# Query-major exponentials of an attention backward pass by DMA transpose instead of a second matmul and exp

## The chip, the cores and the metric

The kernel runs on one core of a Trainium2 chip. The metric is the device time of one execution in microseconds (us), as the median of several runs. Before the change it is 2852.1 us, from two runs of 2850.25 and 2853.94 us.

## What is computed

A block of a network with its gradients. The forward part is `out = x + s * g`, where `s` is multi-head attention (32 heads of width 16, 2048 rows, model width 512) on the layer-normed input, and `g` is the SiLU of a two-layer MLP. The kernel returns `out` and the gradients with respect to `x` and the six weights and biases, for a given gradient of `out`. All inputs and outputs are bf16.

```
xn = layernorm(x)
q, k, v = split(xn @ wqkv)                       # 32 heads of 16
p = softmax(q @ k.T / 4)                         # 2048 x 2048 for each head
s = (p @ v) @ wo
g = silu(gelu(layernorm(xn) @ w1 + b1) @ w2 + b2)
out = x + s * g
grads = vjp of out for (x, wqkv, wo, w1, b1, w2, b2)
```

The change touches the attention's part alone. Its backward pass needs the matrix of exponentials in two orientations. With keys on the partitions ("key-major") it serves the sums over keys: the output, the row sums and the gradient of q. With queries on the partitions ("query-major") it serves the sums over queries: the gradients of k and v.

## The kernel before, in words

There are three phases: `phase_pre` (norms, MLP, projections; the first attention step follows at about 285 us), `attention_core`, and `phase3` (weight gradients; from about 2257 us). `attention_core` is emitted in an order written out by hand (a manual schedule), and each engine runs its own instructions in that order.

**Loops.** Two heads are worked on at a time, so there are 16 pairs. For each pair there are four query chunks `qc` of 512 queries: 64 blocks `j`. Each block has 16 steps `kb`, one for each 128 keys: 1024 steps `g`, and 19 more at the end to drain. Sixteen steps after the key-major work of a block ("a unit") its query-major work ("b unit") runs: also 16 units, numbered by a key chunk `kc` of 512 keys and a query group `qb` of 128 queries. The Z matmuls of a b unit come another `lagb` = 3 steps later.

**The a unit of a step.** L648 `s`: two matmuls of scores into a PSUM tile. L676 `et`: ACT's exponential of both heads into a bf16 tile that holds four steps (`etp`, 3 tiles). L662 `d`: two matmuls. L697 `gts`: VectorE multiplies `d` by `et` into a tile that holds two steps (`gtp`, 4 tiles). L729, L732, L744: matmuls that sum over keys into `X`. Every second step, L710: SyncE (SP) issues one DMA transpose of the whole `gts` tile, 128x2048, into half of a `gk` tile (`gbp`).

**The b unit of a step.** L634 `t`: two matmuls of the same scores with the queries on the partitions. L684 `e`: ACT's exponential of them. L807: Z matmuls with `e`. L813: Z matmuls with `gk`. After the fourth `qb` of a `kc`, L818 or L820 adds Z to `acc`. For the units named in `dma_units`, here (1, 3) and (3, 3), two of the 16, `t` and `e` are left out: after the last of the four steps that fill an `et` tile, L716 issues a DMA transpose of a quarter of it, 128x1024, into an `ek` tile (`ekp`), and L807 reads that instead.

**Queues.** All DMAs of this phase go through SP's queue: L710, L716, and for each pair the loads L585 to L587, the transposes L594 and L602 of the operands KVT and QDT, and the store L827. SP issues in order, and a transpose that has to wait holds up those behind it. A tile of a pool is written again when its last reader is done. In the order of emission, `emit_dmat(g)` stands ahead of `emit_z(g - lagb, ...)` in a step, so a step's transposes are emitted before its Z matmuls.

Of the kernel before, what the change touches and what calls it, by code (L numbers as in the profile page):

```python
# [541 lines left out]

def attention_core(ctx, tc, NAT_s, NATQ_s, Oall, dQall, dKVT_out, ident_f32, npairs=16, nqc=4):
    nc = tc.nc
    dma_units = ((1, 3), (3, 3))
    lagb = 3
    sb = lambda name, bufs: ctx.enter_context(tc.tile_pool(name=name, bufs=bufs))
    opnd = sb("opnd", 1)
# [3 lines left out]
    ps_z = ctx.enter_context(tc.tile_pool(name="ps_z", bufs=1, space=PSUM))  # L552
    etp = sb("etp", 3)
    gtp = sb("gtp", 4)
    gbp = sb("gbp", 6)
    ekp = sb("ekp", 4)
    ep = sb("ep", lagb + 2)
    xsp = sb("xsp", 1)
    finp = sb("finp", 2)
# [306 lines left out]
def full_kernel(ctx, tc, A_x, A_wqkv, A_wo, B_x, B_w1, B_b1, B_w2, B_b2, grad_out,  # L866
# [32 lines left out]
    with ExitStack() as cO:  # L899
        pO = cO.enter_context(tc.tile_pool(name="persistO", bufs=1))  # L900
        k.Oall = pO.tile([128, NT, D], bf16, name="Oall")
        k.dQall = pO.tile([128, NT, D], bf16, name="dQall")
        if "att" in phases:
            with ExitStack() as cB:
                with tc.manual_schedule():
                    attention_core(cB, tc, k.NAT_s, (k.NATQq_s, k.NATQd_s), k.Oall, k.dQall, k.dKVT_s, k.ident_f)
        if "3" in phases:
            phase3(ctx, tc, k, A_x, A_wqkv, A_wo, B_w1, B_w2, grad_out, out_0, out_1, out_2, out_3, out_4, out_5, out_6, out_7, dbg)
# [56 lines left out]
```

## Time and profile before

The profiled execution has a span of 2849.1 us; the median of the runs is 2852.1 us.

| engine, whole span | busy us | share | instructions |
|---|---|---|---|
| PE (matmul) | 2397.8 | 84% | 19712 |
| PE weight loads | 845.8 | 30% | 19712 |
| DVE (VectorE) | 2029.7 | 71% | 3382 |
| ACT (ScalarE) | 2057.1 | 72% | 2357 |
| POOL (GpSimd) | 619.0 | 22% | 1023 |

| DMA issue in attention | count | size of one | issue, median us | start of issue to landing, median us |
|---|---|---|---|---|
| gk <- gts, L710 | 512 | 128x2048 bf16 | 1.93 | 4.4 |
| ek <- et, L716 | 128 | 128x1024 bf16 | 1.80 | 3.9 |

How to read the lines that follow: the page cuts the span into 40 equal slices of 71 us and gives the busy share of each in tenths, where 9 means 90% or more. "DMA" is the share of the core's 16 DMA engines. A row of the groups gives line, engine, operation, output<-input, shapes and count, then busy time and the mean duration of one in ns, then the engine's idle time just ahead of these instructions and what ended most of it. The stages view gives for each stretch the busy time and count of each engine, then the granted clock of TensorE, the DMA share, and GB/s.

### The profile page before, as it was taken

What the parts mean: (1) busy time and instruction counts of PE and PEld (TensorE: products, weight loads), DVE (VectorE), ACT (ScalarE), POOL (GpSimd) and SP (SyncE); (2) the same over time, 40 slices, a digit from 0 to 9 for tenths busy, and PEclk for the clock granted to TensorE, in tenths of its full rate; (3) what the DMA queues carried; (4) which work ended last, traced back from release to release, by engine and by line L of the source; (5) the groups of instructions that cost most, each with busy time, mean ns of one, the idle gap of its engine ahead of it and who ended that gap; (6) DMA issues with size and microseconds to landing.
All of it is one profiled execution on the core that took longest, in us unless ns stands there. A gap on an engine that the chain in (4) does not pass through costs nothing. (4 is left out here: it accounts for less than half of the span.)

```text
span 2849.1 us, 50869 instructions
## 1 busy us (share of the span) xinstructions
PE 2397.8 (84%) x19712; PEld 845.8 (30%) x19712; DVE 2029.7 (71%) x3382; ACT 2057.1 (72%) x2357; POOL 619.0 (22%) x1023
## 2 busy tenths in 40 slices
PE   3686999999999999999999999999999857665967
PEld 2332222222222222222222222222222333332443
DVE  5664778878878878878877877888888638880044
ACT  2342799999999999999999999999999634440020
POOL 0434101111111110101101111110101227870024
PEclk8898799999999999999999999999999978887989
DMA  5434889999999999999899999999999753326431
GB/s 177 107 126 128 156 161 184 159 179 172 167 180 159 181 166 174 174 164 182 156 182 171 167 183 154 183 168 170 177 164 159 191 164 103 97 83 160 115 130 42
DMA packets 1426198, 442.86 MB, mean 155 GB/s; under 512 B 1349281, under 2 KB 1410082, under 8 KB 1425954
## 3 DMA queue, kind: packets, MB, share of 16 engines
q1 hardware_dynamic: 1352562, 385.98, 72.9%
q10 hardware_dynamic: 73392, 53.62, 6.2%
q8 instruction: 154, 2.52, 0.3%
q14 instruction: 90, 0.74, 0.1%
HBM read 65.41 MB, written 55.32 MB: 42 GB/s over the span
## 5 line engine op out<-in xcount | busy, mean ns | idle before, releaser
L697 DVE TENSOR_TENSOR gts<-d,et 128x512 bf16<-128x512 f32 x2048 | 1315.0, 683 | 374.6 <-ACT et L676 146.4
L676 ACT ACTIVATE et<-s 128x1024 bf16<-128x1024 f32 x1024 | 1058.1, 1056 | 11.8 <-PE d L662 11.7
L684 ACT ACTIVATE e<-t 128x1024 bf16<-128x1024 f32 x896 | 933.9, 1043 | 165.0 <-PE t L634 163.9
L662 PE MATMUL d<-QDT,KVT 32*128 32x512 bf16 x2048 | 492.4, 382 | 30.5 <-DVE gts L697 28.5
L648 PE MATMUL s<-QDT,KVT 32*128 32x512 bf16 x2048 | 402.9, 385 | 135.7 <-ACT et L676 120.3
L729 PE MATMUL X<-et,Lc 128*32 128x512 bf16 x2048 | 405.3, 392 | 14.1 <-DVE xs L750 14.1
L732 PE MATMUL X<-et,NAT 128*32 128x512 bf16 x2048 | 405.5, 393 | 0.0
L744 PE MATMUL X<-gts,NAT 128*17 128x512 bf16 x2048 | 400.7, 388 | 0.0
L813 PE MATMUL Z<-gk,W 128*32 128x512 bf16 x2048 | 394.2, 379 | 0.0
L807 PE MATMUL Z<-e,W 128*32 128x512 bf16 x1792 | 351.3, 387 | 2.8 <-DVE acc L820 2.0
L634 PE MATMUL t<-KVT,QDT 32*128 32x512 bf16 x1792 | 349.9, 382 | 2.3 <-ACT e L684 2.3
L777 POOL TENSOR_TENSOR W<-NATQd,rL 128x128 bf16<-128x128 bf16 x64 | 25.7, 401 | 1386.0 <-DVE rL L772 1386.0
L648 PEld LDWEIGHTS <-KVT 32*128 32x128 bf16 x2048 | 146.9, 91 | 399.3 <-issue 397.8
L634 PEld LDWEIGHTS <-QDT 32*128 32x128 bf16 x1792 | 103.9, 91 | 365.7 <-issue 365.7
L744 PEld LDWEIGHTS <-NAT 128*17 128x17 bf16 x2048 | 93.0, 88 | 338.5 <-issue 338.5
L729 PEld LDWEIGHTS <-Lc 128*32 128x32 bf16 x2048 | 104.3, 93 | 216.2 <-issue 216.2
L820 DVE TENSOR_TENSOR acc<-Z,acc 64x512 f32<-64x512 f32 x192 | 129.0, 672 | 13.0 <-PE Z L813 13.0
L807 PEld LDWEIGHTS <-W 128*32 128x32 bf16 x2048 | 121.3, 93 | 55.3 <-issue 53.8
L662 PEld LDWEIGHTS <-KVT 32*128 32x128 bf16 x2048 | 108.1, 91 | 9.4 <-issue 1.0
L825 POOL CAST ob<-acc 64x512 bf16<-64x512 f32 x64 | 38.7, 605 | 313.3 <-DVE acc L820 311.3
L813 PEld LDWEIGHTS <-W 128*32 128x32 bf16 x2048 | 103.9, 96 | 7.5
L732 PEld LDWEIGHTS <-NAT 128*32 128x32 bf16 x2048 | 99.3, 94 | 14.5
(200 smaller groups left out, 2600.2 us busy)
## 6 DMA issues: line engine op xcount, KB each, us to landing
gk<-gts SPq DMA_TRANSPOSE x512, 4.4
HG_s<-hg SPq DMA_DIRECT2D x16, 448.0 KB, 3.0
DH_s<-dh ACTq DMA_DIRECT2D x16, 448.0 KB, 2.5
NAT<-NAT_s SPq DMA_DIRECT2D x16, 264.0 KB, 3.1
GB_s<-gB ACTq DMA_DIRECT2D x16, 256.0 KB, 2.0
dKVT_s<-ob SPq DMA_DIRECT2D x16, 256.0 KB, 3.8
dhc<-DH_s ACTq DMA_DIRECT2D x2, 2048.0 KB, 13.9
w_sb<-in_B_w_dram SPq DMA_DIRECT2D x2, 1792.0 KB, 14.8
```

Of the source, the lines that this page charges most:

```text
L634: nc.tensor.matmul(t[:, hj, :], lhsT=op["QDT"][r:r + 32, q0:q0 + 128], rhs=op["KVT"][r:r + 32, kc * 512:(kc + 1) * 512], start=True, stop= ...
L648: nc.tensor.matmul(s[:, hj, :], lhsT=op["KVT"][r:r + 32, kb * 128:(kb + 1) * 128], rhs=op["QDT"][r:r + 32, qc * 512:(qc + 1) * 512], start ...
L662: nc.tensor.matmul(d[:], lhsT=op["KVT"][r:r + 32, kb * 128:(kb + 1) * 128], rhs=op["QDT"][r:r + 32, qc * 512:(qc + 1) * 512], start=True, ...
L676: nc.scalar.activation(out=et[:, :, kb % 4, :, :].rearrange("k b h q -> k h b q"), in_=st_s.pop(g)[:].rearrange("k h (b q) -> k h b q", b= ...
L684: nc.scalar.activation(out=e[:], in_=st_t.pop(g)[:], func=ACT.Exp)
L697: nc.vector.tensor_tensor(out=gts[:, kb % 2, hj, :].rearrange("k (b q) -> k b q", b=4), in0=ds[hj][:].rearrange("k (b q) -> k b q", b=4), ...
L729: nc.tensor.matmul(X[64 + 32 * hj:96 + 32 * hj, :], lhsT=Lc[:], rhs=et[:, :, kb % 4, hj, :], start=(kb == 0), stop=False, skip_group_check ...
L732: nc.tensor.matmul(X[32 * hj:32 * hj + 32, :], lhsT=NATt[:, kb, hj, 1:33], rhs=et[:, :, kb % 4, hj, :], start=(kb == 0), stop=(kb == 15), ...
L744: nc.tensor.matmul(X[64 + 32 * hj:64 + 32 * hj + 17, :], lhsT=NATt[:, kb, hj, 0:17], rhs=gts[:, kb % 2, hj, :], start=False, stop=(kb == 1 ...
L807: nc.tensor.matmul(Z[32 * hj:32 * hj + 32, :], lhsT=blk[j]["W1"][:, qb, hj, :], rhs=ev[:, hj], start=(qb == 0), stop=False, tile_position= ...
L813: nc.tensor.matmul(Z[32 * hj:32 * hj + 32, :], lhsT=blk[j]["W2"][:, qb, hj, :], rhs=gv[:, :, :, hj, qb, :], start=False, stop=(qb == 3), t ...
L820: nc.vector.tensor_tensor(out=av, in0=Z[0:64, :], in1=av, op=ALU.add)
```

## The change

Three lines of `attention_core`. `dma_units` now names all 16 units of a block, so `emit_t` and `emit_exp_b` do nothing (L634 and L684 have no instruction any more), `emit_dmat` issues four `ek` transposes after each fourth step instead of one after each eighth, and all Z matmuls of L807 read `ek`. The pool `ekp` grows from 4 to 20 tiles and `gbp` shrinks from 6 to 5. The pool `ep` stays, unused. The arithmetic is otherwise the same.

```diff
 def attention_core(ctx, tc, NAT_s, NATQ_s, Oall, dQall, dKVT_out, ident_f32, npairs=16, nqc=4):
     nc = tc.nc
-    dma_units = ((1, 3), (3, 3))
+    dma_units = tuple((kc, qb) for kc in range(4) for qb in range(4))
     lagb = 3
...
     etp = sb("etp", 3)
     gtp = sb("gtp", 4)
-    gbp = sb("gbp", 6)
-    ekp = sb("ekp", 4)
+    gbp = sb("gbp", 5)
+    ekp = sb("ekp", 20)
     ep = sb("ep", lagb + 2)
```

## The prediction

> **What bounds the kernel now.** I read the page's slices first, then the costliest groups, then the busy time by stretch, and last the DMA queues of the attention stage alone. All durations are from one profiled execution with a span of 2849.1 us; the median of the runs is 2852.1, so I add 3 us at the end.
>
> The slices, and from the groups the rows that the change touches:
> ```profile
> PE   3686999999999999999999999999999857665967
> DVE  5664778878878878878877877888888638880044
> ACT  2342799999999999999999999999999634440020
> DMA  5434889999999999999899999999999753326431
> GB/s 177 107 126 128 156 161 184 159 179 172 167 180 159 181 166 174 174 164 182 156 182 171 167 183 154 183 168 170 177 164 159 191 164 103 97 83 160 115 130 42
> ...
> L697 DVE TENSOR_TENSOR gts<-d,et 128x512 bf16<-128x512 f32 x2048 | 1315.0, 683 | 374.6 <-ACT et L676 146.4
> L676 ACT ACTIVATE et<-s 128x1024 bf16<-128x1024 f32 x1024 | 1058.1, 1056 | 11.8 <-PE d L662 11.7
> L684 ACT ACTIVATE e<-t 128x1024 bf16<-128x1024 f32 x896 | 933.9, 1043 | 165.0 <-PE t L634 163.9
> ...
> L634 PE MATMUL t<-KVT,QDT 32*128 32x512 bf16 x1792 | 349.9, 382 | 2.3 <-ACT e L684 2.3
> ...
> gk<-gts SPq DMA_TRANSPOSE x512, 4.4
> ```
> Attention runs from about 288 to 2257 us: 1969 us, 1043 steps, 1.89 us each. PE, ACT and the DMA engines all show 9 there, so three candidates stand side by side. The stretches separate them (columns: busy of PE, weight load, DVE, ACT, POOL; granted clock, DMA share, GB/s). First the whole stage; then a stretch in which DMAs are queued up without a pause; then one that holds a single gk transpose; then one with gk, ek, gk in a row:
> ```profile
> 288.00:2257.00 1969.00, 1798.09 (x16395) 549.96 (x16395) 1566.56 (x2626) 1789.68 (x1921) 267.14 (x699) 0.99 0.97 171
> 575.40:607.88 32.48, 30.04 (x277) 9.07 (x278) 26.00 (x44) 29.29 (x32) 3.04 (x9) 1.00 1.15 195
> ```
> ```profile
> 1228.70:1231.40 2.70, 2.48 (x22) 0.64 (x20) 2.43 (x5) 1.92 (x3) 0.00 (x0) 1.00 1.02 194
> 1232.30:1239.00 6.70, 5.88 (x54) 1.93 (x51) 6.33 (x14) 6.01 (x7) 2.74 (x8) 1.00 1.05 198
> ```
> ACT is what sets a step today: it is busy 1790 of 1969 us, 91% (its instructions overlap by about a tenth, so the two groups' sum, 1992, is larger), and the waits of L676 sum to 11.8 us. PE is close behind. The DMA engines are nearer to their end than anything says in words: the share of 0.97 is a sum of packet times that overlap, so it is not the ceiling. In the queued-up stretch the same column reads 1.15, at 195 GB/s, and other such stretches of 32 to 43 us read 192 to 196 GB/s. **That is the ceiling: about 195 GB/s.** The stage moves 171, 88% of it. The reader should take two things from this: ACT is the limit by a small margin, and the resource to which the change moves the work has one eighth left.
>
> **What the Trainium skill says.** "Advanced Engine Details and Errata", section X-Bar Transpose (TRN2), expects 350-400 GB/s of a transposing DMA; "DMA: Bandwidth & Descriptors", section Latency and other measured facts, has 261 GB/s with a non-contiguous middle dimension. The trace agrees with neither: 195 GB/s, in packets of which 1,349,281 of 1,426,198 are under 512 B. The measurement decides; the pages' figures serve as a rival below. "Perfetto Trace Analysis", section DMA Instruction — HWDGE, says that a DMA instruction's time in the profile ends with its issue and that the movement lies outside it; the trace agrees: a gk's issue takes 1.93 us in the median and it lands 4.4 us after its start.
>
> **The change part by part.**
> - Removed, PE: 1792 matmuls of L634, 349.9 us, with their weight loads. PE in the stage goes from 1798 to 1448 us. Worth nothing on the end if DMA is the bound.
> - Removed, ACT: 896 exponentials of L684, 933.9 us. What stays in the stage is L676, at most 1058 us. This was the limit, so the next one is what counts: DVE, 1567 us of work, all of it kept; PE 1448; and DMA.
> - Added, DMA: ek transposes from 128 to 1024, so 896 x 128x1024 bf16 = 896 x 262,144 B = 234.9 MB, all on SP's queue. The DMA view cut to the stage says 336.73 MB now, of which some 4.7 MB are loads of the next stage that start in its last 15 us: 332 + 235 = 567 MB. At 195 GB/s that is 2907 us. **This is the path.** Nothing covers it: the DMA engines already were at 88%, and the work beside it (DVE 1567) is far shorter.
> - The same from single transposes: the 194 GB/s x 2.70 us above are 524 KB, one gk, so at most 2.7 us and by its packets 2.6; gk, ek, gk fit in 6.7 us, so an ek adds about 1.4. Four steps need 2 gk and 4 ek: 2 x 2.6 + 4 x 1.37 = 10.7 us, against 4 x 1.89 = 7.5 us now. 256 such groups make 2739; the KVT and QDT transposes of 15 pairs 30 x 2.6 = 78; their loads 15 x 0.54 MB / 195 = 42; 16 stores 22; total 2881. The 16 KB instruction fetches that ride on the same engines (128 in the stage) are in the first sum, not in this one. The two agree within 1%. I take 2905.
> - Unknown: an ek behind an ek does not occur before. From below, half a gk in a run of gk (2.46 / 2 = 1.23); from above, SP's issue time, 1.80 us median plus 0.09 between two, 1.89. Unhindered issues of 1.25 occur with the queue full, so issue can keep pace; I take 1.37. The ends change the stage by 768 x (-0.14) = -108 and, SP limited, see the second rival.
> - gbp 6 to 5: a gk tile is claimed at step 4m+1, and the tile five earlier is last read by Z at step 4m+2, one step later. So SP's first gk of a group waits for PE, and the second gk and the four ek's of that group are queued behind it. It costs nothing while compute is ahead of the DMAs by over a step, and it will be: gts has 4 tiles of two steps and et 3 of four, so the engines may lead by a whole group of transposes before they block. If compute did not lead, it would cost a step and the 1.2 us from issue to first packet.
> - ekp 4 to 20: five groups of 4; a tile's last Z read is one step ahead of its reuse. No wait.
> - Late next: DVE and ACT will stand idle for their buffers, L697 for gts and L676 for et, both freed by transposes. Z reads its ek 16 steps after it was made, so PE does not wait there.
>
> Sum: outside the stage 2849.1 - 1969 = 880; stage 2905; the first packets start some 4 us into it, and the tail has no t and e any more, -5. Span 3784 to 3800, plus 3: **3800 us**.
>
> **Rivals.**
> 1. *SP's issuing is the bound.* For: medians of 1.80 (ek) and 1.93 (gk). A group takes 4 x 1.89 + 2 x 2.02 = 11.6 us, 2970 for all, with loads and stores 3060; total 880 + 3060 = 3940. Against: issues of 1.25 to 1.32, and where they are longer, they end with the transfer ahead.
> 2. *The gk wait bites:* SP stands until PE has done the later step, and the DMA engines run dry once a group: up to 256 x (1.6 + 1.2) = 717 more, 4500. Against: the lead worked out above.
> 3. *Faster:* the transposes run at the pages' 350-400 GB/s when fed without pause. Then 567 MB take 1420 to 1620 us, DVE sets the stage at 1567 to 1700, and the kernel takes 2450 to 2600. It is decided by one number: over 567 / 1969 = 288 GB/s the change gains, under it it loses. At 261 it would be 3055. Against: between 1216 and 1246 us, taken by half microseconds, none with queued transposes shows over 222 GB/s, but for a microsecond of catch-up after a stall (266).
> 4. *The change leaves t and e in place:* ruled out, since in the changed program no instruction stands at L634 or L684.
>
> **How the numbers follow.** Transfer-bound near 195 GB/s (3680 to 3880): 0.74. SP bound or a mix with it (3880 to 4050): 0.16. Gk wait or other gaps (over 4050): 0.05. Pages' rates: 0.05, of which 0.03 faster. The range 3680 to 3980 holds the first case and most of the second. A measurement of this kernel can tell about 2% from no change; nothing lies near that line, so same gets 0.01.
>
> **What would show it.** Right: GB/s near 190-200 through all of the stage, DMA share at about 1.15 throughout, ACT down to some 3 or 4 tenths and DVE to 5, the step at 2.8 us, L697 and L676 idle behind DMA. SP bound: GB/s under 185 with ek issues at 1.8 us end to end. Gk wait: holes in the DMA traffic once in four steps and SP waiting for PE at L710. I am wrong if the stage's rate leaves 185 to 205 GB/s, or if DVE stays busy over 70% of it.

## The result, and the profile after

The changed kernel takes 3826.6 us in the median (3825.1 to 3828.1), against 2852.1 us: a ratio of 1.342, with a 95% interval of 1.338 to 1.346. The profiled execution has a span of 3823.3 us. The forecast was 3800 us, with a range of 3680 to 3980.

The slices of the page of the changed kernel, and four of its costliest groups:
```profile
PE   5777767776767676767777777777777776676678
ACT  3433333333333333333333333333333332344020
PEclk8986777776777877777777777777776777888889
DMA  5349999999999999999999999999999999432641
GB/s 166 108 127 185 194 192 193 196 193 194 193 193 194 194 195 195 195 195 195 196 192 195 194 194 192 195 195 195 193 192 196 193 195 208 152 97 82 157 142 38
...
L697 DVE TENSOR_TENSOR gts<-d,et 128x512 bf16<-128x512 f32 x2048 | 1312.7, 683 | 1259.6 <-DMA gk<-gts 939.7
L676 ACT ACTIVATE et<-s 128x1024 bf16<-128x1024 f32 x1024 | 1005.4, 1023 | 1899.2 <-PE d L662 1111.4
...
L662 PE MATMUL d<-QDT,KVT 32*128 32x512 bf16 x2048 | 785.1, 497 | 539.6 <-DVE gts L697 529.0
...
L807 PE MATMUL Z<-ek,W 128*32 128x512 bf16 x2048 | 518.0, 501 | 10.9 <-DMA ek<-et 8.2
```
The GB/s row was uneven before, between 154 and 191 in the slices of attention. Now it stands at 192 to 196 in nearly all of them, as a resource at its ceiling would. L697 waited 375 us before, 257 of them for ACT or PE; it now waits 1260 us, and 940 of them end with the landing of a gk, which frees a `gts` tile. L807, which reads the new ek tiles, waits 11 us in all. So no consumer is late; the producers stand still for their buffers.

The same stage in the stages view (columns as before: PE, weight load, DVE, ACT, POOL; clock, DMA share, GB/s), and the waits of SP's own queue (total, times, longest):
```profile
288.00:3216.00 2928.00, 2101.88 (x14593) 479.80 (x14594) 1567.95 (x2621) 1002.55 (x1022) 268.35 (x698) 0.74 1.09 194
```
```profile
SPq L710 <- PE d L662: 222.8, 141, 3.3
...
SPq L710 <- PE s L648: 129.2, 53, 3.5
SPq L716 <- ACT et L676: 115.6, 167, 2.0
SPq L710 <- PE X L744: 69.8, 48, 2.3
```
The span grew by 974 us: 959 of it in the attention stage (2928 against 1969), 15 in the phase after it. DVE's work in the stage is what it was, 1568 us; ACT's fell from 1790 to 1003. SP does wait for PE at L710, 422 us in all, where the kernel before has no such wait; the prediction worked it out for the smaller `gbp`, which was not tried apart. But in the records of the DMA packets of the stage, the gaps of over 0.1 us between packets come to 12 us altogether (207 us in the kernel before): the queued transfers cover that wait.

The same records show what the 194 GB/s is made of. For 159 us of the stage, in 197 stretches of mostly about 1 us, packets still come but the rate, averaged over 0.25 us, is under 40 GB/s. Of the 175 fetches of instructions by DMA in the stage, 170 have such a stretch begin within 2.5 us of them, though these 2.5 us cover only 15% of the stage. So the rate is a mean with stalls in it, most of them beside an instruction fetch; whether the fetch is the cause was not tried. The first gk of a group, the one that waits for PE, has 36 us of these stalls, and the second, which does not, has 28: little room for a cost of that wait.

### The profile page after: what moved, and what is told of

Same layout as the page of the kernel before. It is cut to its first block, busy times and chain, and to the rows that moved or that the text cites. A ratio compares the mean times of both kernels' runs of the same rounds, so it can differ in the third digit from the quotient of the medians.

```text
span 3823.3 us, 47091 instructions
## 1 busy us (share of the span) xinstructions
PE 2709.7 (71%) x17920; PEld 779.4 (20%) x17920; DVE 2035.0 (53%) x3382; ACT 1272.9 (33%) x1461; POOL 621.5 (16%) x1023
## 5 line engine op out<-in xcount | busy, mean ns | idle before, releaser
L697 DVE TENSOR_TENSOR gts<-d,et 128x512 bf16<-128x512 f32 x2048 | 1312.7, 683 | 1259.6 <-DMA gk<-gts 939.7
L676 ACT ACTIVATE et<-s 128x1024 bf16<-128x1024 f32 x1024 | 1005.4, 1023 | 1899.2 <-PE d L662 1111.4
L662 PE MATMUL d<-QDT,KVT 32*128 32x512 bf16 x2048 | 785.1, 497 | 539.6 <-DVE gts L697 529.0
L729 PE MATMUL X<-et,Lc 128*32 128x512 bf16 x2048 | 540.5, 523 | 181.1 <-ACT et L676 177.4
L648 PE MATMUL s<-QDT,KVT 32*128 32x512 bf16 x2048 | 492.6, 477 | 109.5 <-ACT et L676 96.0
L732 PE MATMUL X<-et,NAT 128*32 128x512 bf16 x2048 | 529.8, 511 | 0.0
L807 PE MATMUL Z<-ek,W 128*32 128x512 bf16 x2048 | 518.0, 501 | 10.9 <-DMA ek<-et 8.2
L813 PE MATMUL Z<-gk,W 128*32 128x512 bf16 x2048 | 524.0, 505 | 0.0
L744 PE MATMUL X<-gts,NAT 128*17 128x512 bf16 x2048 | 515.7, 499 | 0.2 <-DVE gts L697 0.2
L662 PEld LDWEIGHTS <-KVT 32*128 32x128 bf16 x2048 | 126.7, 95 | 579.1 <-issue 578.6
L807 PEld LDWEIGHTS <-W 128*32 128x32 bf16 x2048 | 123.9, 98 | 37.9 <-issue 27.6
L813 PEld LDWEIGHTS <-W 128*32 128x32 bf16 x2048 | 114.8, 106 | 17.0 <-issue 15.7
L762 DVE COPY xt<-XT 128x512 f32<-128x512 f32 x64 | 44.3, 692 | 89.2 <-PE XT L760 89.2
L427 PE MATMUL ps_dy<-w1T,dh1T 128*128 128x512 bf16 x224 | 75.1, 477 | 1.0 <-ACT dh1T L422 0.3
```

What stands on the lines that cost most here:

```text
L427: nc.tensor.matmul(ps[:], lhsT=dh1T[:, fc, :], rhs=w1T[:, fc, :], start=(fc == 0), stop=(fc == FC - 1))
L648: nc.tensor.matmul(s[:, hj, :], lhsT=op["KVT"][r:r + 32, kb * 128:(kb + 1) * 128], rhs=op["QDT"][r:r + 32, qc * 512:(qc + 1) * 512], start ...
L662: nc.tensor.matmul(d[:], lhsT=op["KVT"][r:r + 32, kb * 128:(kb + 1) * 128], rhs=op["QDT"][r:r + 32, qc * 512:(qc + 1) * 512], start=True, ...
L676: nc.scalar.activation(out=et[:, :, kb % 4, :, :].rearrange("k b h q -> k h b q"), in_=st_s.pop(g)[:].rearrange("k h (b q) -> k h b q", b= ...
L697: nc.vector.tensor_tensor(out=gts[:, kb % 2, hj, :].rearrange("k (b q) -> k b q", b=4), in0=ds[hj][:].rearrange("k (b q) -> k b q", b=4), ...
L729: nc.tensor.matmul(X[64 + 32 * hj:96 + 32 * hj, :], lhsT=Lc[:], rhs=et[:, :, kb % 4, hj, :], start=(kb == 0), stop=False, skip_group_check ...
```

## The experiments

Two questions were put to the chip. Is it the transfers' bytes that set the 2928 us, or SP's issuing, or the wait of the first gk? And was ACT really what bounded the kernel before, as the prediction read it?

### e1: half of the units

```diff
-    dma_units = tuple((kc, qb) for kc in range(4) for qb in range(4))
+    dma_units = tuple((kc, qb) for kc in range(4) for qb in (1, 3))
-    ekp = sb("ekp", 20)
+    ekp = sb("ekp", 10)
```


> Eight of the 16 units of a block go by transpose, the other eight keep t and e (ekp 10). Transfer theory: 512 fewer ek transposes are 134 MB less, so (566 - 134) MB at 194.8 GB/s give a stage of about 2220 us and a kernel of 3110 us (3080 to 3140), still well over the 2852 of before, with 192 to 197 GB/s in the stage. Rival, SP's issuing: a group of four steps issues 2 x 1.42 + 2 x 2.33 = 7.5 us, 1920 us in all, which the exponentials hide: about 2870 us. Rival, the gk wait or the lower TensorE clock: nearly all of the loss stays, over 3500 us.

Measured: 3124.5 us, 1.096 (1.091 to 1.101) of the kernel before. Its stage:
```profile
288.00:2520.00 2232.00, 1919.25 (x15573) 494.20 (x15573) 1553.33 (x2619) 1479.62 (x1529) 266.43 (x696) 0.89 1.12 194
```
Same 194 GB/s, fewer bytes, a stage of 2232 us: the time follows the bytes. The three rivals that foresaw 2870 or over 3500 us fall. But the number of transposes falls with the bytes here; e2 and e3 change the one without the other.

### e2: one transpose where there were four

```diff
-            for qb in range(4):
-                if (kc, qb) in dma_units:
-                    ek = ekp.tile([128, 8, 128], bf16, name="ek")
-                    blk[j]["Ek"][(kc, qb)] = ek
-                    nc.sync.dma_start_transpose(out=ek[:], in_=st_et[g][:, qb]...)
+            ek = ekp.tile([128, 4, 8, 128], bf16, name="ek")
+            for qb in range(4):
+                blk[j]["Ek"][(kc, qb)] = ek
+            nc.sync.dma_start_transpose(out=ek[:]..., in_=st_et[g][:]...)
```
`ekp` is 5 here, and L807 reads its quarter of the long tile.

> The four ek transposes of an et tile are issued as one of 128x4096: same bytes, 256 issues in place of 1024. Transfer theory with bytes alone: no change from 3826 us (3780 to 3830). Transfer theory with a fixed part in each transpose (an ek takes 1.39, a gk 2.50 us, so 0.28 fixed): 768 x 0.28 = 215 less, 3610 us. SP's issuing as the bound: 768 x 1.42 = 1090 us of issue time less, under 2900 us unless the long issue grows in proportion.

Measured: 3680.3 us, 1.291 (1.285 to 1.297). The stage, and the issue of the long transpose (min/median/max in ns):
```profile
295.00:3070.00 2775.00, 2041.79 (x14554) 471.45 (x14548) 1562.33 (x2617) 1003.34 (x1020) 267.58 (x698) 0.76 1.14 204
```
```profile
L715 SPq DMA_TRANSPOSE ek<-et x256: 4726/5194/6365, 297.8 to 3065.5; - x128
```
The bytes are the same and 146 us are gone, 0.19 us for each of the 768 seams between transposes that no longer exist; the rate rises from 194 to 204 GB/s. That lies between the two transfer expectations. The run does not decide against SP's issuing, though. The expectation set a condition, "unless the long issue grows in proportion", and it did: 5.19 us in the median, 3.9 times the 1.33 us of a single ek in the changed kernel. So the 0.19 us may belong to the data or to SP.

### e3: the same count, half the bytes

```diff
-                    ek = ekp.tile([128, 8, 128], bf16, name="ek")
-                    nc.sync.dma_start_transpose(out=ek[:], in_=st_et[g][:, qb]...)
+                    ek = ekp.tile([128, 4, 128], bf16, name="ek")
+                    nc.sync.dma_start_transpose(out=ek[:], in_=st_et[g][:, qb, 0:2]...)
```
Each matmul of L807 becomes two of 256 columns that both read that half, so the other half is missing from the sum; where qb = 0, L813 now comes first.

> Still 1024 ek transposes, but each moves half (128x512), so 134 MB less; the Z matmuls read that half twice, so part of the sum is left out, in four matmuls of 256 columns in place of two of 512. Transfer theory: with bytes alone 3826 - 134 MB / 194.8 GB/s = 3137 us; with 0.28 us fixed in each, 1024 x 0.555 less, 3260 us. If the issue of 1.25 + 0.09 us becomes the floor of these short ones: 4 x 1.34 + 2 x 2.0 = 9.4 us a group, 3300 to 3400 us. SP's issuing as the bound of the changed kernel: no change, 3826 us.

Measured: 3742.6 us, 1.313 (1.307 to 1.319). **None of the four numbers was right.** The stage, then a stretch with two gk and the start of the first ek, then one with the last three ek of a group; below, the issue of an ek:
```profile
292.00:3133.00 2841.00, 2049.84 (x16616) 608.34 (x16611) 1565.45 (x2619) 1013.24 (x1021) 267.49 (x698) 0.76 0.84 152
1007.00:1012.60 5.60, 3.39 (x36) 0.95 (x32) 2.89 (x5) 2.95 (x3) 0.06 (x1) 0.97 1.11 210
1012.70:1016.60 3.90, 3.90 (x39) 1.19 (x36) 2.80 (x6) 1.02 (x1) 0.61 (x1) 0.62 0.50 101
```
```profile
L716 SPq DMA_TRANSPOSE ek<-et x1024: 1198/1264/2509, 296.9 to 3131.9; - x171
```
The same row of the changed kernel:
```profile
L716 SPq DMA_TRANSPOSE ek<-et x1024: 1233/1330/2882, 295.2 to 3212.7; - x171
```
The DMA share says it: 1.11 while gk are moved, 0.50 while ek are. In the packets of the second stretch an ek of 128x512 flows for 0.77 us and one starts every 1.31 us, which is the issue of 1.26 and the step to the next. So these short transposes are paced by SP. The group comes to more than the 9.4 us that I had worked out because I let SP issue ahead during the gk's; it does not get far ahead. The first ek of a group is issued only when the second gk is already being moved, and the others after it, so the 2.5 us of each gk and the 1.31 us of each ek come one after the other. For the changed kernel this means that its ek's (1.40 us from end to end behind one another) lie only 0.09 us above this issue floor: **transfers and SP's issuing are nearly in balance there**. That the transfers are ahead by this little is seen in the packets: in the changed kernel an ek starts to flow before the ek ahead of it has ended in 761 of 768 cases, in e3 in 23. Halving the bytes of the ek's alone took 84 us off, where the bytes alone would have taken 689.

### e4: no gk

```diff
-            nc.sync.dma_start_transpose(out=blk[j]["Gk"][kc][:, h], ...)   # L710
-            nc.tensor.matmul(Z[...], lhsT=blk[j]["W2"][...], rhs=gv[...])  # L813
```


> The changed kernel without the gk transposes and without the Z matmuls that read them: that part of the sum is left out. 268 MB less, 298 MB are left. Transfer theory: the DMA engines need 298 / 0.195 = 1530 us and are no longer alone; DVE's 1573 us of work sets the stage at 1650 to 1800, the kernel at 2530 to 2700 us, and DVE is busy over 85% of the stage. If something other than transfers set the 2925 us (ek issues of 1.42 us x 1024 = 1454 us do not, nor do they here), such as the lower TensorE clock, the kernel stays over 3300 us.

Measured: 2541.0 us, 0.892 (0.886 to 0.897). The stage:
```profile
288.00:1945.00 1657.00, 1484.38 (x12581) 321.89 (x12580) 1540.81 (x2631) 1048.01 (x1028) 268.14 (x699) 0.95 1.05 183
```
This kernel leaves out the part of the sum that the gk carry. DVE is busy 1541 of 1657 us, 93%: with half the bytes taken off, the engine that the prediction named as the next bound is nearly full. But 183 GB/s is nearly all that ek's alone allow, since a 128x1024 every 1.40 us is 187 GB/s; the run does not tell the two apart. All 1024 ek transposes are still there.

### e5, e6, e7: none, three and four units by transpose

These are the kernel before with `dma_units` changed, to test what bounded it:
```diff
-    dma_units = ((1, 3), (3, 3))
+    dma_units = ()                                    # e5
+    dma_units = ((0, 3), (1, 3), (3, 3))              # e6, ekp 6
+    dma_units = ((0, 3), (1, 3), (2, 3), (3, 3))      # e7, ekp 6
```


> The kernel before with no unit by transpose (dma_units empty): 128 exponentials and 256 t matmuls more, 33.5 MB less to move. If ACT bounds the kernel before: 128 x 0.92 to 1.04 = 118 to 133 us more, 2970 to 2985 us. If the DMA engines already bound it: faster, about 2850 - 33.5 / 0.195 = 2680 us or at least not slower.

> The kernel before with three units of 16 by transpose (ekp 6). ACT bound: 64 exponentials less, 59 to 67 us less, 2785 to 2793 us, as the DMA engines would need only (332 + 17) / 0.195 = 1790 us. DMA engines already in the way through their bursts: 2840 to 2930 us.

> The kernel before with four units of 16 by transpose, one for each key chunk (ekp 6). ACT bound: 118 to 133 us less, but the DMA engines then need (332 + 34) / 0.195 = 1875 us of a stage of 1969, so at best 2852 - 94 = 2758; I expect 2760 to 2820 us. If the transfers' waits already cost: no gain, 2850 to 2900 us.

The stage with none and with four units:
```profile
288.00:2257.00 1969.00, 1804.90 (x16651) 566.57 (x16651) 1573.47 (x2624) 1892.21 (x2048) 268.00 (x699) 0.99 0.85 154
288.00:2257.00 1969.00, 1788.07 (x16115) 532.21 (x16115) 1560.15 (x2621) 1680.48 (x1790) 266.77 (x697) 0.99 1.07 188
```
Measured: 2850.3 us (0.9995 of the kernel before, 0.9988 to 1.0002), 2850.7 us (0.9993, 0.9980 to 1.0006) and 2848.7 us (0.9987, 0.9977 to 0.9996). **Between none and four units the time moves by 0.1% at most**, though ACT's work in the stage goes from 1892 us of 1969 (96%) with none to 1680 with four. ACT's work alone therefore does not set the time with two units; at none, with 96%, it may, which no run shows. The rows of e, in the attention stage, for none, two (the kernel before) and four units show where the saved exponentials went:
```profile
L684 ACT ACTIVATE e<-t 128x1024 bf16<-128x1024 f32 x1024 | 1082.7, 1058 | 63.4 <-PE t L634 63.0
```
```profile
L684 ACT ACTIVATE e<-t 128x1024 bf16<-128x1024 f32 x896 | 933.9, 1043 | 165.0 <-PE t L634 163.9 <-ACT et L676 0.2
```
```profile
L684 ACT ACTIVATE e<-t 128x1024 bf16<-128x1024 f32 x768 | 793.5, 1033 | 274.8 <-PE t L634 274.8
```
Each exponential left out adds (274.8 - 63.4) / 256 = 0.83 us of waiting for the next t. The order of PE around such a step in the kernel before shows why (start, duration, instruction):
```profile
1214.01 0.39 PE L648 MATMUL s<-QDT,KVT 32*128 32x512 bf16 x2
1214.16 0.37 PE L662 MATMUL d<-QDT,KVT 32*128 32x512 bf16 x1
1214.76 0.37 PE L662 MATMUL d<-QDT,KVT 32*128 32x512 bf16 x1 [0.23 <-DVE gts L697]
1215.06 0.39 PE L744 MATMUL X<-gts,NAT 128*17 128x512 bf16 x2
1215.35 0.39 PE L807 MATMUL Z<-e,W 128*32 128x512 bf16 x2
1215.56 0.39 PE L813 MATMUL Z<-gk,W 128*32 128x512 bf16 x2
1215.89 0.39 PE L634 MATMUL t<-KVT,QDT 32*128 32x512 bf16 x2
```
The step has no t of its own. Its second d waits for DVE to free a PSUM buffer, and the next step's t stands behind it, X and Z on PE and comes at 1215.89. ACT had nothing to do for 0.78 us before the e at 1216.38, most of the 0.9 us that it had saved.

### e8, e9, e10: the next t ahead of d

If that is the cause, moving one matmul pair ahead of d, X and Z must free the time. This edit is on the kernel before, with two, three and four units:
```diff
-        emit_t(g)
+        if g not in st_t:
+            emit_t(g)
...
         emit_s(g + 1)
+        b = b_unit(g)
+        if b is not None and b[1:] in dma_units:
+            emit_t(g + 1)
         emit_d(g)
```


> The kernel before (two units of 16 by transpose), with one matmul pair moved: in a step whose own unit has no t, the next step's t is emitted ahead of d instead of after z. Theory: what a left-out exponential saves on ACT (0.9 us) is paid back because the next t stands on PE behind d, and d waits for gts on DVE to free its PSUM buffer; moved ahead, t is there in time, the 164 us in which L684 waits for t fall under 80, and up to 128 x 0.8 = 100 us go: 2750 to 2800 us. Rival: the pace is DVE's or PE's own, and the wait only moves to another row: 2840 to 2860 us.

> The same move with three units by transpose. Theory: up to 192 x 0.8 = 154 us less than the three units without it (2851), bounded by ACT's 1740 us of the stage and by 349 MB / 194.8 = 1790 us of transfers: 2700 to 2790 us. Rival: no change, 2840 to 2860 us.

> The same move with four units by transpose. The transfers now need 363 MB / 194.8 = 1865 us of the stage's 1969, so at most 105 us can go: 2750 to 2800 us, and not faster than three units. Rival: no change, 2840 to 2860 us.

Measured: 2808.3 us (0.983 of the kernel before, 0.982 to 0.985), 2788.4 us (0.976, 0.973 to 0.979) and 2792.7 us (0.978, 0.976 to 0.980). The stages of e9 and e10, cut at their shorter end; then the rows of e in e8 and e9, and of t in e8:
```profile
288.00:2190.00 1902.00, 1751.64 (x16238) 510.23 (x16239) 1569.45 (x2622) 1751.91 (x1854) 266.23 (x697) 0.99 1.07 185
288.00:2190.00 1902.00, 1744.52 (x16049) 486.42 (x16041) 1565.42 (x2617) 1700.46 (x1781) 262.75 (x689) 0.98 1.11 192
```
```profile
L684 ACT ACTIVATE e<-t 128x1024 bf16<-128x1024 f32 x896 | 940.2, 1050 | 106.2 <-PE t L634 105.0 <-ACT et L676 0.2
L684 ACT ACTIVATE e<-t 128x1024 bf16<-128x1024 f32 x832 | 870.2, 1047 | 115.8 <-PE t L634 115.6
L634 PE MATMUL t<-KVT,QDT 32*128 32x512 bf16 x1792 | 349.8, 382 | 45.0 <-ACT et L676 42.7 <-ACT e L684 2.3
```
The place of t is shown to be a cause: the wait for t falls from 164 to 105 us with two units, and the time with it. It is not shown to be the whole one. Two units gain 47 us against the runs of the kernel before beside them, of up to 100 that I expected, and the wait stays above the 80 us that I gave: t now waits for ACT to free its own buffer, 43 us in all. Three units (2776 to 2792 us) and four (2789 to 2800) cannot be told apart for certain; four are no faster, as foreseen, and e10's stage moves 192 GB/s, close to the 194 of the changed kernel. **e9 is faster than both kernels**, by 2.4% against the one before.

## Why the prediction was right

- **The ceiling of 195 GB/s**, read from stretches of 32 us in which DMAs were queued, holds for 2928 us: 194 GB/s. The stage was put at 2905 us by bytes and took 2928; the bytes were put at 567 MB, and the DMA view of the stage counts 567.3. This one step carried the number. That 195 was right to 1% is in part luck, as it is the mean of a mix and no constant. The stretch shown of before held nine gk's and two ek's; its gk's took 2.74 us in the mean (191 GB/s), because two of them stalled and took 3.4 and 3.7. In the changed kernel the gk's take 2.52 us in the mean (208 GB/s) and the far more numerous ek's 1.43 (183 GB/s): by chance these come to nearly the same rate. With longer transposes the same bytes went at 204 GB/s (e2), with shorter ones fewer bytes at 152 (e3). The prediction's step from GB/s to time was sound only because the ek's were long enough.
- **ek behind ek**, unknown before, was taken as 1.37 us and is 1.40 in the median of the 762 such pairs in the packet records that follow within 0.05 us. Its upper end, SP's 1.89 us, did not come: the issue's median fell from 1.80 to 1.33 us.
- **SP's issuing as a rival**: the price of 3940 us was too high, and the packets, which flow almost without a gap, show that data sets the pace. But e3 shows a floor of 1.31 us close under it. The prediction's sentence that issue can keep pace was true by 0.09 us for each ek, a margin that it had not worked out: luck again.
- **The gk wait** exists (422 us of SP's time) and costs little that can be seen, as argued from the lead that `gts` and `et` allow: 12 us of gaps.
- **Faster, at 350 to 400 GB/s:** no run came over 204 GB/s over its stage.
- **Idle engines**: L697 waits for gk as named. L676's idle time is put mostly to PE's d, which itself waits for L697; its direct wait for ek is 710 us.
- **Where it was wrong without harm:** "ACT is what sets a step today". Taking 128 exponentials out of the kernel with two units, or putting 128 in, changed next to nothing (e7, e5). ACT was 91% busy, but its idle time was in part a wait for a t that stood behind d on PE, as e8 to e10 show; the rest of the loop that kept the time where it was stays open. The sum did not use that reading, because ACT's saving was priced at nothing.
- The rest outside the stage was taken as unchanged and grew by 15 us, all after attention; why was not looked into.
- **The sum itself:** 880 + 2905 + 4 - 5 + 3 is 3787 us. The 3800 that was forecast has some 13 us more, for which the prediction gives no term; they stand for no mechanism and made the number look closer by as much.

## What to carry to other kernels

Before work is moved to the DMA engines, find a stretch in which they have a queue, and read its GB/s: that is near the ceiling for transfers of those sizes, and the mean share of the stage (0.97 here, with 12% to spare) is not. Then divide the new bytes by it, and look at what SP pays for each issue, since the short transposes of e3 were paced by that instead. And an engine that is 91% busy need not be the bound: change its work a little, and if the time does not move, look for the wait that grew by as much.

## What the runs showed of the hardware

- The granted TensorE clock fell where PE had less to do: 0.99 in the stage of the kernel before, 0.89 in e1, 0.74 in the changed kernel, whose L662 matmuls last 497 ns instead of 382. The Trainium skill, "TensorE: Matmul & The Clock Gate", Part 1, has PE at half its clock after an idle window of some 3.4 us; the trace fits, with waits of L662 for gts of up to 5.2 us and stretches at 0.50. It was not tried apart. That the stage of e1 at 0.89 and of the changed kernel at 0.74 both move 194 GB/s gives no sign that it cost time there.
- The shortest issue of a transpose on SP grows little with its size up to 128x2048: 1.20 us for 128x512, 1.23 for 128x1024, 1.34 for 128x2048. For 128x4096 it was 4.73. In the changed kernel, where transfers are queued, the issue of a gk takes 2.24 us in the median.
- Longer transposes moved more: 152 GB/s in the stage with 128x512 ek's, which SP paced, 194 with 128x1024, 204 with 128x4096.
- Beside 170 of the 175 instruction fetches in the stage of the changed kernel, the transposes' rate fell under 40 GB/s, for about 1 us each time.
